# On-chip copies of keys by ScalarE and GpSimd in place of DMAs, later identities and a retuned order, in an attention and two-FFN kernel

## The chip, the cores and the metric

The kernel runs on one core of a Trainium2 chip. The metric is the device time of one execution in microseconds. Before the change the median of 3 runs is 525.11 us (524.25 to 525.11).

## The reference

Attention comes first: q, k and v are (2 batches, 8 heads, 768 positions, 64). Each query sees the keys of the last 128 positions, itself included, and the first 4 keys of its batch. Then two feed-forward blocks over the 1536 x 512 rows that result:

```python
scores = scale * q @ k.T; keep = is_sink | in_window
a = exp(scores - max); a = a / (sum(a) + 1e-9); x = a @ v      # heads side by side: 1536 x 512
h = x @ w_in                                                   # 512 -> 1024
solu = h * softmax(h)
ln = (solu - mean) / sqrt(var + 1e-6) * g_ln
x = ln @ w_out                                                 # 1024 -> 512
h = x @ w2_in                                                  # 512 -> 2048
r = relu(h); out = (r * r) @ w2_out                            # 2048 -> 512
```

Inputs and output are float32 arrays; the weights arrive as raw 64-bit words that the kernel converts on the chip.

## The kernel before, in words

**Precision.** A float32 operand is split into a high and a low float16 part, and a product is three matmuls (high by high, high by low, low by high). So every operand is prepared twice: ScalarE (ACT) or VectorE (DVE) writes the high part, TensorE (PE) subtracts it again with a scaled negative identity (`negq`, `neg1`, `negp`; lines L610, L476), and ACT or DVE writes what is left, the low part.

**Tiles.** There are 12 tiles of 128 queries, six to a batch, called t = 0 to 11. A tile's scores have up to 260 columns: its own 128 keys, 4 sink keys, and the 128 keys of the tile before. For each tile `prep_q` and `prep_k` turn q and k with transposes on PE (L592, L594) and build the tiles `qs` and `ks`, which hold high and low parts stacked over the two halves of the partitions. Tile 0 is built in halves by ACT from PSUM. For t = 1 and later the second halves are copies from partitions 64 to 127 into 0 to 63 or back: three DMAs of queries (L657, L659, L661; the third reads what the first writes), three of keys (L701, L703, L705), one 128 x 1024 DMA of the previous tile's keys (L714), and a small GpSimd (POOL) copy of the sink keys (L712). `prep_v` clips v and splits it (`vs`; L725 to L736). Then come the eight heads (scores L789, a custom DVE pass with the row's maximum L799, exponentials on ACT L804), the transposes of the probabilities, their split, the product with v (L866), and the division by the sums (`xs`, L886).

**First and second FFN.** `first(t)` (L957) multiplies the turned attention rows `xh`/`xl` by w_in, `norm(t)` forms solu and its moments (L1000 to L1020, with one power step on POOL, L1018, and the scaled result `so` by POOL, L1020), and `second(t)` (L1046) multiplies by w_out. Weights come in units: craw10 to craw13 for w_in, craw20 to craw23 for w_out, 1 MB each (L504, L506), which DVE converts in three passes of 128 x 1024 (L431, L433, L435); then ACT writes the high part and PE and ACT the low part (L475 to L478). The second FFN's units w3x follow the same way at about 255 us and later (low part by DVE, L466), in 16 steps of `h2` (L1080), `square` (L1093, `gh` L1097, `gl` L1100) and `o2` (L1117), each for four groups of columns. `gl` may go to DVE or POOL.

**Who sets the order.** The kernel's generators ask for an engine with an estimated time, and a list scheduler, `Order`, issues on the host the ask that can start earliest by these estimates; of asks that are ready by the time the engine is free the one with the lowest key goes first. The keys stand in the table at L32 to L50. All engines run their instructions in the order written, and SP issues nearly all DMAs, in order: an SP instruction that waits holds all DMAs behind it. The loads of tile 0's k and q have the fixed key -50; the load of gains is asked with key 0, a weight unit with its entry of `C_KEY`. The four scaled identities (L242) are made by POOL before everything that it is asked for later. `dg` (L563) are eight diagonal matrices on POOL that turn the gain into a matmul.

Of the kernel before, what the change touches and what calls it, by code (L numbers as in the profile page):

```python
# [17 lines left out]
ALU = mybir.AluOpType  # L18
# [13 lines left out]
PE_W = (17.45, 21.36, 14.67, 76.35, 72.53, 117.36, 72.01, 5.72)  # L32
PE_T = (-40.11, 93.82, 0.88, 1.8, -18.4)
LEAD = 41.26
C_KEY = (-13.78, -119.36, -163.11, -72.69, -17.51, -197.67, -111.51, 11.15)
W_AT = (-21.55, 118.65)
K_W = -173.85
K_HEAD = (6.34, 33.8, 152.98, 26.26)
K_TURN = (13.58, 52.57, -0.0)
K_PV = (32.41, -132.48)  # L40
K_PREPK = (-83.35, 152.22, -72.32)
K_PREPQ = (6.35, 247.73, 58.74)
K_PREPV = (38.93,)
K_LOAD = 119.08
K_FIRST = (-16.04, 28.03, 17.79)
K_NORM = 20.87
K_LNT = (-123.17, -36.52)
K_SECOND = (19.15, -1.15, -46.7)
A_0 = (-25.54, -32.74, -19.99, -9.44)
F_0 = (44.96, -4.33, -33.57, -14.12)  # L50
# [157 lines left out]
def attention_moe_moe2(ctx: ExitStack, tc: tile.TileContext, q, k, v, n_sink, window,  # L208
# [32 lines left out]
    for dst, by in ((negq, -1.0 / QSC), (idw, WSC), (neg1, -1.0), (negp, -1.0 / PSC)):  # L241
        nc.gpsimd.tensor_scalar(dst, ident, by, None, ALU.mult)  # L242
# [44 lines left out]
    with tc.manual_schedule():  # L287
# [182 lines left out]
        def low_w(l, x, h, by):  # L470

            for c in range(2):
                yield take("L")
                yield PE, 1.1
# [77 lines left out]
        def load_gsb():  # L552
# [7 lines left out]
            for i in range(CF):  # L560
                if PE_W[CM + i // 2] > 0:
                    yield POOL, 0.3
                    nc.gpsimd.tensor_scalar(dg[:, i], ident, gsw[:, i:i + 1], None, ALU.mult)  # L563
            post("dg")

# [40 lines left out]
        def low_part(t, kind, dst, tr, hi, by, scale=1.0):  # L606

            if less(t, kind):
                yield PE, 0.23
# [10 lines left out]
        HALVES = ((slice(0, 64), slice(64, 128), 0), (slice(64, 128), slice(0, 64), 1))  # L620

        def prep_q(t):
# [3 lines left out]
            for n, h0, h1 in parts(t):  # L626
# [5 lines left out]
                if t < NDIR:  # L632
                    yield ACT, 2 * act_us(512 * sh)
                    for r, o, a in HALVES:
                        nc.scalar.activation(qs[r, 0, a, ps_], tv[r], AF.Copy, scale=QSC)
                    yield PE, 0.3 * sh
# [19 lines left out]
            yield SP, 0.5  # L656
            nc.sync.dma_start(qs[0:64, :, 1], qs[64:128, :, 0])  # L657
            yield SP, 0.5, 2.0
            nc.sync.dma_start(qs[64:128, :, 1], qs[64:128, :, 0])  # L659
            yield SP, 0.5, 2.0  # L660
            nc.sync.dma_start(qs[64:128, :, 0], qs[0:64, :, 0])  # L661
            post(("q", t, 0))

        def prep_k(t):
# [8 lines left out]
            for n, h0, h1 in parts(t):  # L673
# [5 lines left out]
                if t < NDIR:  # L679
                    yield ACT, 2 * act_us(512 * sh)  # L680
                    for r, o, a in HALVES:
                        nc.scalar.activation((k0, k1)[a][r, ps_], tv[r], AF.Copy, scale=QSC)
                    yield PE, 0.3 * sh
# [10 lines left out]
            if t >= NDIR:  # L694
# [5 lines left out]
                yield SP, 0.5, 2.0  # L700
# [747 lines left out]
```

## Time and profile before

| what | value |
|---|---|
| median of 3 runs | 525.11 us |
| the profiled execution | 523.43 us, span 521.6 us |
| PE busy | 492.5 us, 94% of the span |
| DVE busy | 353.4 us, 68% |
| ACT busy | 297.8 us, 57% |
| POOL busy | 105.3 us, 20% |
| granted clock of PE | 0.996 of full speed on average |

The span is what the profiler saw of the core; 1.8 us of the execution lie outside it. Busy shares are averages over stages with different limits: in the first 80 us weights are converted while tiles 0 to 2 go through, in 80 to 260 us attention and the first FFN alternate on PE, around 260 to 280 us the kernel goes over to the second FFN, and from 280 us on there is the second FFN alone.

### The profile page before, as it was taken

The numbers are of one execution on the slowest core, as the hardware profiler recorded it, in microseconds if no ns is written. First come the engines' busy times: TensorE is split into PE (matmuls) and PEld (weight loads), VectorE is DVE, ScalarE is ACT, GpSimd is POOL, SyncE is SP. The second block draws the span as 40 slices with busy tenths as digits, with TensorE's granted clock in tenths as the row PEclk, the third lists the DMA queues.
The fourth block names the chain that finished last, engine by engine and source line by source line (L and its number), as shares of the span: only waits on it lengthen the run. The fifth ranks groups of instructions, "written<-read, shape, count | busy, mean of one in ns | idle before, by whom it ended". The sixth has DMA issues, their size and how long they took to land.

```text
span 521.6 us, 10644 instructions
## 1 busy us (share of the span) xinstructions
PE 492.5 (94%) x4022; PEld 317.1 (61%) x4022; DVE 353.4 (68%) x819; ACT 297.8 (57%) x658; POOL 105.3 (20%) x190
## 2 busy tenths in 40 slices
PE   4779989999999999999988999999999999999993
PEld 2345568878887888787764555555555555555551
DVE  3788958976776687689899898733475444763223
ACT  6768977777766776564534343567645655322221
POOL 3813753352604222122300000000000000110000
PEclk9999999999999999999999999999999999999998
DMA  6998794444353318003345444677889997000003
GB/s 177 303 268 246 151 233 91 95 92 92 78 113 84 85 42 271 1 18 109 119 147 177 162 165 165 234 268 280 321 313 333 372 330 243 0 2 1 1 0 128
DMA packets 91180, 82.31 MB, mean 158 GB/s; under 512 B 60656, under 2 KB 81264, under 8 KB 88944
## 3 DMA queue, kind: packets, MB, share of 16 engines
q1 hardware_dynamic: 90976, 81.55, 51.5%
q8 instruction: 33, 0.54, 0.5%
q14 instruction: 27, 0.22, 0.1%
q10 hardware_dynamic: 144, 0.00, 0.0%
HBM read 69.28 MB, written 3.15 MB: 139 GB/s over the span
## 4 chain that ended last, share of the span: by engine, by line
PE 80%; DMA 7%; DVE 5%; POOL 3%; ACT 2%; issue 1%; SPq 1%; POOLq 0%; DVEq 0%; ACTq 0%
PE ps L1080 24%; PE ps L1117 23%; PE ps L1046 10%; PE ps L957 10%; PE ps L594 6%; PE ps L789 3%; PE ps L866 3%; DMA craw<-in_moe_w_in_dram 2%; DMA craw<-in_moe_w_out_dram 2%; DMA vraw<-in_v_dram 1%; DVE cx L433 1%; DMA ks<-ks 1%; PE ps L592 1%; DMA qraw<-in_q_dram 1%; POOL vs L736 1%
## 5 line engine op out<-in xcount | busy, mean ns | idle before, releaser
L1093 DVE SCALAR_TENSOR_TENSOR gf<-ps,relu 128x384 f32<-128x384 f32 x64 | 35.5, 555 | 75.4 <-ACT relu L1090 70.8
L1090 ACT ACTIVATE relu<-ps 128x384 f32<-128x384 f32 x64 | 31.3, 489 | 92.4 <-PE ps L1080 92.4
L1080 PE MATMUL ps<-x2h,w34l 128*128 128x384 f16 x256 | 83.5, 326 | 0.0
L1080 PE MATMUL ps<-x2l,w34h 128*128 128x384 f16 x256 | 83.4, 326 | 0.0
L1080 PE MATMUL ps<-x2h,w34h 128*128 128x384 f16 x256 | 83.4, 326 | 0.0
L1080 PEld LDWEIGHTS <-w34h 128*128 128x128 f16 x512 | 49.7, 98 | 38.4
L1117 PE MATMUL ps<-w34h,gh 128*128 128x512 f16 x192 | 72.8, 379 | 0.0
L1117 PE MATMUL ps<-w34h,gl 128*128 128x512 f16 x192 | 72.8, 379 | 0.0
L1117 PE MATMUL ps<-w34l,gh 128*128 128x512 f16 x192 | 72.8, 379 | 0.0
L1046 PE MATMUL ps<-lnh,w2h 128*128 128x128 f16 x384 | 68.2, 219 | 1.3 <-DVE facb L1157 1.3
L1046 PE MATMUL ps<-lnl,w2h 128*128 128x128 f16 x384 | 68.1, 219 | 1.1 <-DVE lnl L616 1.1
L1046 PE MATMUL ps<-lnh,w2l 128*128 128x128 f16 x384 | 68.1, 219 | 0.0
L1046 PEld LDWEIGHTS <-w2h 128*128 128x128 f16 x768 | 61.3, 98 | 5.6 <-issue 1.7
L1117 PEld LDWEIGHTS <-gh 128*128 128x128 f16 x384 | 37.5, 98 | 38.6
L1100 POOL TENSOR_TENSOR gl<-gf,gh 128x384 f16<-128x384 f32 x10 | 9.6, 956 | 202.6 <-ACT gh L1097 202.6
L804 ACT ACTIVATE pp<-neg,bias_all 128x260 f32<-128x260 f32 (+1 forms) x96 | 46.9, 491 | 5.0 <-DVE bias_all L799 3.8
L1097 ACT CAST gh<-gf 128x384 f16<-128x384 f32 x64 | 32.5, 508 | 29.1 <-DVE gf L1093 29.1
L799 DVE CUSTOM_DVE_ANT_0 neg<-ps,m 128x260 f32<-128x260 f32 (+1 forms) x96 | 36.6, 397 | 14.5 <-PE ps L789 8.8
L1100 DVE TENSOR_TENSOR gl<-gf,gh 128x384 f16<-128x384 f32 x54 | 30.0, 556 | 19.6 <-ACT gh L1097 19.6
L1046 PEld LDWEIGHTS <-w2l 128*128 128x128 f16 x384 | 37.6, 98 | 1.2 <-issue 1.2
L789 PE MATMUL ps<-ks,qs 128*128 128x260 f16 (+1 forms) x192 | 35.5, 269 | 2.2 <-DVE bias_all L799 1.6
L957 PE MATMUL ps<-w1h,xh 128*128 128x512 f16 x96 | 36.4, 379 | 0.1
(230 smaller groups left out, 1020.7 us busy)
## 6 DMA issues: line engine op xcount, KB each, us to landing
craw<-in_moe_w_in_dram SPq DMA_DIRECT2D x16, 512.0 KB, 5.3
craw<-in_moe_w_out_dram SPq DMA_DIRECT2D x16, 512.0 KB, 4.7
qs<-qs SPq DMA_DIRECT2D x33, 128.0 KB, 3.4
craw<-in_moe_w_in_dram SPq DMA_DIRECT2D x4, 1024.0 KB
craw<-in_moe_w_out_dram SPq DMA_DIRECT2D x4, 1024.0 KB, 5.8
crawx<-in_q_dram SPq DMA_DIRECT2D x3, 1024.0 KB, 5.8
crawx<-in_k_dram SPq DMA_DIRECT2D x3, 1024.0 KB, 7.4
crawx<-in_v_dram SPq DMA_DIRECT2D x3, 1024.0 KB, 8.2
```

The costliest lines, as they stand in the source:

```text
L594: nc.tensor.transpose(out, src, ident)
L789: nc.tensor.matmul(o, QS[t][:, x, a, p, :], KS[t][:, a, p, 0:w], start=(x == 0), stop=(x == 1))
L799: nc.vector.tensor_tensor_reduce(neg[:, 0:w], o, m, scale=-0.125 / (QSC * QSC), scalar=3.0e38, op0=ALU.add, op1=ALU.min, accum_out=bias)
L804: nc.scalar.activation(pp[:, a, 0:w], neg[:, 0:w], AF.Exp, bias=bias, scale=-1.0, accum_out=SUMS[t][:, j:j + 1])
L957: nc.tensor.matmul(bank(B_H + hh), l[:, c, :], r[:, c, hh * 512:(hh + 1) * 512], start=(c == 0 and k == 0), stop=(c == CM - 1 and k == 2))
L1046: nc.tensor.matmul(o[:, ms], l[:, c, ms], ln[r][:, c % 4, :], start=(n == 0), stop=(n == 12 * CF - 1))
L1080: nc.tensor.matmul(o, l[:, c, :], r[gi][:, c, xs], start=(k == 0), stop=(k == 3 * CM - 1))
L1090: nc.scalar.activation(tt, o, AF.Relu, scale=G2SC / (X2SC * WSC) ** 2)
L1093: nc.vector.scalar_tensor_tensor(gf, o, 0.0, tt, ALU.max, ALU.mult, accum_out=gsum[:, n:n + 1])
L1097: nc.scalar.copy(gh, gf)
L1100: (nc.gpsimd if eng == POOL else nc.vector).tensor_tensor(gl, gf, gh, ALU.subtract)
L1117: nc.tensor.matmul(ps[:, ACC[m]], l[:, ms], r, start=(f == 0 and i == 0), stop=(f == CF2 - 1 and i == 2))
```

## The change

A new generator `move` copies within the chip. Its kind says what: 0 queries, 1 the tile's own keys, 2 the previous tile's keys. Below the threshold T_COPY[kind] for the tile number t it asks for ACT, DVE or POOL, whichever the scheduler can start first, else it issues a DMA as before. With the thresholds given, queries stay on DMA for all tiles, the own keys are copied by an engine for t = 1 alone (three copies of 64 x 512), and the previous tile's keys for all ten tiles that have one (128 x 1024). In the order that results the three copies of t = 1 stand on ACT and the ten of the previous keys on POOL. The identities are made by a step of their own behind POOL's index steps (`scaled`), and what reads them waits for it. The fixed key of tile 0's loads becomes K_LOAD0. The estimates for a DMA issue (0.5 to 0.65) and for `dg` (0.3 to 0.6) change, and so does every key in the table. All 64 `gl` stand on POOL in the new order (10 of 64 before, the others on DVE), and both steps of the low part of v on POOL for the two tiles that had it on DVE (L733).

```diff
-PE_W = (17.45, 21.36, 14.67, 76.35, 72.53, 117.36, 72.01, 5.72)
...
-C_KEY = (-13.78, -119.36, -163.11, -72.69, -17.51, -197.67, -111.51, 11.15)
...
+T_COPY = (-16.61, 1.23, 22.13)
+K_LOAD0 = -3.08
+PE_W = (59.84, 31.21, 13.49, 50.01, 33.64, 206.75, 96.92, 28.53)
...
+C_KEY = (-26.92, -150.49, -222.09, -92.67, 7.82, -175.79, -155.85, 9.24)
...
-    for dst, by in ((negq, -1.0 / QSC), (idw, WSC), (neg1, -1.0), (negp, -1.0 / PSC)):
-        nc.gpsimd.tensor_scalar(dst, ident, by, None, ALU.mult)
...
+        def scaled():
+            for dst, by in ((negq, -1.0 / QSC), (idw, WSC), (neg1, -1.0), (negp, -1.0 / PSC)):
+                yield POOL, 0.53
+                nc.gpsimd.tensor_scalar(dst, ident, by, None, ALU.mult)
+            post("scaled")
...
+        def move(t, kind, dst, src, n, last=True):
+
+            if t < T_COPY[kind]:
+                eng = yield (ACT, 0.2 + n * 0.00083), (DVL, 0.15 + n / 3840.0), (POOL, 0.2 + n * 0.001)
+                (nc.scalar.copy if eng == ACT else (nc.gpsimd if eng == POOL else nc.vector).tensor_copy)(dst, src)
+            else:
+                yield (SP, 0.65, 2.0) if last else (SP, 0.65)
+                nc.sync.dma_start(dst, src)
...
-                nc.sync.dma_start(k1[64:128], k0[64:128])
-                yield SP, 0.5
-                nc.sync.dma_start(k1[0:64], kl[64:128])
-                yield SP, 0.5, 2.0
-                nc.sync.dma_start(k0[64:128], kl[0:64])
+                yield from move(t, 1, k1[64:128], k0[64:128], 512)
+                yield from move(t, 1, k1[0:64], kl[64:128], 512, False)
+                yield from move(t, 1, k0[64:128], kl[0:64], 512)
...
-                yield SP, 0.75, 2.0
-                nc.sync.dma_start(ks[:, :, :, P + NSK:].rearrange("p a c n -> p (a c) n"), ks0[:, :, :, 0:P].rearrange("p a c n -> p (a c) n"))
+                yield from move(t, 2, ks[:, :, :, P + NSK:].rearrange("p a c n -> p (a c) n"), ks0[:, :, :, 0:P].rearrange("p a c n -> p (a c) n"), 1024)
...
+        start(-60.0, scaled())
...
-                    att(b + K_LOAD + n if t or nm == "v" else -50 + 3 * n + 4 * part[0], load(nm, src, t, *part))
+                    att(b + K_LOAD + n if t or nm == "v" else K_LOAD0 + 3 * n + 4 * part[0], load(nm, src, t, *part))
```

SP's first ten DMAs before; kraw0 and qraw0 are tile 0's keys and queries, in halves, par the window's size:

```order
L318 DMA kraw0_140<-in_k_dram 128x4x64
L323 DMA par_67<-in_window_dram 128x2
L318 DMA qraw0_141<-in_q_dram 128x4x64
L318 DMA kraw0_140<-in_k_dram 128x4x64
L318 DMA qraw0_141<-in_q_dram 128x4x64
L504 DMA craw10_157<-in_moe_w_in_dram 128x2048
L554 DMA gsb_93<-in_moe_g_ln_dram 128x8x1
L318 DMA kraw1_145<-in_k_dram 128x8x64
L318 DMA qraw1_146<-in_q_dram 128x8x64
L504 DMA craw11_217<-in_moe_w_in_dram 128x2048
```

The same ten places now:

```order
L323 DMA par_67<-in_window_dram 128x2
L505 DMA craw10_149<-in_moe_w_in_dram 128x2048
L318 DMA kraw0_136<-in_k_dram 128x4x64
L318 DMA qraw0_137<-in_q_dram 128x4x64
L555 DMA gsb_89<-in_moe_g_ln_dram 128x8x1
L318 DMA kraw0_136<-in_k_dram 128x4x64
L505 DMA craw11_167<-in_moe_w_in_dram 128x2048
L318 DMA qraw0_137<-in_q_dram 128x4x64
L318 DMA kraw1_141<-in_k_dram 128x8x64
L318 DMA qraw1_142<-in_q_dram 128x8x64
```

The first weight unit stands ahead of tile 0's keys, and the second one among tile 0's halves; in both the rows follow the program's start.

PE at the first heads of tile 1 before, with the semaphores that each row waits for; DMAHW names a DMA queue:

```order
L475 MATMUL ps_61<-cx12_334,idw_71 128x512 [waits Activation_49]
L476 LDWEIGHTS neg1_68
L476 MATMUL ps_61<-w1h_117,neg1_68 128x512
L592 MATMUL ps_61<-ident_62,kraw2_225 128x128 [waits DMAHW4_49]
L592 MATMUL ps_61<-ident_62,kraw2_225 128x128 x3
L789 LDWEIGHTS qs1_148 [waits DMAHW1_49,DMAHW7_49,DVE_49,DMAHW6_49]
L789 MATMUL ps_61<-ks1_147,qs1_148 128x260 [waits Pool_49]
L789 LDWEIGHTS qs1_148
L789 MATMUL ps_61<-ks1_147,qs1_148 128x260
```

The same place now:

```order
L801 LDWEIGHTS qs1_144 [waits DMAHW4_49]
L801 MATMUL ps_61<-ks1_143,qs1_144 128x260 [waits DVE_49]
L801 LDWEIGHTS qs1_144
L801 MATMUL ps_61<-ks1_143,qs1_144 128x260
L801 LDWEIGHTS qs1_144 [waits DMAHW1_49,DMAHW0_49]
L801 MATMUL ps_61<-ks1_143,qs1_144 128x260 [waits DVE_49]
L801 LDWEIGHTS qs1_144
L801 MATMUL ps_61<-ks1_143,qs1_144 128x260
L476 MATMUL ps_61<-cx12_352,idw_71 128x512 [waits DVE_49]
```

The heads stand ahead of the low part of unit craw12 (before: behind it and behind the transposes of kraw2, L592), and wait for fewer DMA queues: those of the queries alone.

POOL ahead of the power step of tile 0's norm (st0) before; vs4 is the split of tile 4's v, so0 the scaled result that PE turns next:

```order
L725 TENSOR_SCALAR vraw4_596<-vraw4_596 128x512
L810 COPY snk2_576<-pp2_2_751 128x4x4
L730 TENSOR_SCALAR vs4_784<-vraw4_596 128x512
L735 TENSOR_SCALAR vraw4_596<-vraw4_596 128x512
L736 TENSOR_TENSOR vs4_784<-vraw4_596,vs4_784 128x512
L1018 TENSOR_TENSOR st0_753<-st0_753,half_95 128x1
L810 COPY snk2_576<-pp2_2_751 128x4x4
L1020 TENSOR_SCALAR so0_808<-so0_808,st0_753 128x1024
```

The same place now, with the program's new line numbers (L1018 is L1030, L1020 is L1032):

```order
L737 TENSOR_SCALAR vraw4_580<-vraw4_580 128x512
L742 TENSOR_SCALAR vs4_755<-vraw4_580 128x512
L822 COPY snk2_591<-pp2_2_746 128x4x4
L747 TENSOR_SCALAR vraw4_580<-vraw4_580 128x512
L748 TENSOR_TENSOR vs4_755<-vraw4_580,vs4_755 128x512
L822 COPY snk2_591<-pp2_2_746 128x4x4
L822 COPY snk2_591<-pp2_3_805 128x4x4
L1030 TENSOR_TENSOR st0_707<-st0_707,half_91 128x1
L1032 TENSOR_SCALAR so0_815<-so0_815,st0_707 128x1024
```

The split of vs4 keeps its place ahead of the power step, and two copies of sink probabilities (snk2) came between them.

## Rows read from the trace of the kernel before

**Rows 1.** The page, busy time of each engine.

```profile
PE 492.5 (94%) x4022; PEld 317.1 (61%) x4022; DVE 353.4 (68%) x819; ACT 297.8 (57%) x658; POOL 105.3 (20%) x190
```

**Rows 2.** Busy time by stretch: start:end, length, engines, clock, DMA share, GB/s.

```profile
0.00:80.00 80.00, 63.17 (x440) 37.66 (x441) 59.82 (x146) 61.72 (x151) 40.99 (x75) 1.00 0.89 225
4.64:38.30 33.66, 23.89 (x118) 12.54 (x119) 25.19 (x65) 25.82 (x66) 13.88 (x19) 1.00 1.00 273
40.00:66.72 26.72, 25.58 (x181) 15.06 (x180) 24.74 (x51) 23.72 (x56) 12.78 (x17) 1.00 0.83 198
80.00:260.00 180.00, 179.36 (x2167) 145.46 (x2164) 138.87 (x360) 119.94 (x292) 55.64 (x108) 1.00 0.37 93
260.00:280.00 20.00, 16.13 (x159) 10.86 (x158) 19.79 (x30) 7.66 (x13) 2.20 (x2) 1.00 0.48 161
```

**Rows 3.** PE's waits in 0 to 80 us: total, times, longest.

```profile
PE ps L594 <- POOL so L1020: 1.7, 1, 1.7
```

**Rows 4.** Timeline of SP's queue, 0 to 63 us: start, length, DMA issued.

```profile
0.72 0.45 SPq L318 DMA_DIRECT2D kraw<-in_k_dram  x1
...
19.49 0.60 SPq L659 DMA_DIRECT2D qs<-qs  x1
...
20.77 0.70 SPq L504 DMA_DIRECT2D craw<-in_moe_w_in_dram  x1
25.91 0.60 SPq L661 DMA_DIRECT2D qs<-qs  x1
...
28.02 1.23 SPq L506 DMA_DIRECT2D craw<-in_moe_w_out_dram  x1
...
62.92 0.38 SPq L318 DMA_DIRECT2D vraw<-in_v_dram  x1
```

**Rows 5.** DMA issues of the whole run: times, size, median us to landing.

```profile
qs<-qs SPq DMA_DIRECT2D x33, 128.0 KB, 3.4
```

**Rows 6.** Timeline of PE: start, length, instruction, idle before and its releaser.

```profile
3.95 0.66 PE L592 MATMUL ps<-ident,kraw 128*128 128x128 f32 x2 [3.95 <-POOL mtmp L340]
...
31.56 0.39 PE L789 MATMUL ps<-ks,qs 128*128 128x260 f16 x2
...
39.72 0.38 PE L957 MATMUL ps<-w1h,xh 128*128 128x512 f16 x1
...
72.29 0.66 PE L594 MATMUL ps<-ident,so 128*128 128x128 f32 x4 [1.69 <-POOL so L1020]
```

**Rows 7.** Timeline of ACT.

```profile
8.46 0.82 ACT L646 COPY qs<-qs 64x256 f16<-64x256 f16 x2
...
38.30 0.58 ACT L935 CAST xh<-ps 128x512 f16<-128x512 f32 x1 [1.05 <-PE ps L592]
```

**Rows 8.** Timeline of DVE, 10 to 67 us.

```profile
10.92 0.69 DVE L431 TENSOR_SCALAR cx<-craw 128x1024 int32<-128x1024 int32 x1 [1.29 <-DMA craw<-in_moe_w_in_dram]
...
29.21 0.69 DVE L431 TENSOR_SCALAR cx<-craw 128x1024 int32<-128x1024 int32 x1 [0.89 <-DMA craw<-in_moe_w_in_dram]
...
31.20 1.23 DVE L435 SCALAR_TENSOR_TENSOR cx<-craw,cx 128x1024 int32<-128x1024 int32 x1
...
49.91 1.95 DVE L435 SCALAR_TENSOR_TENSOR cx<-craw,cx 128x1024 int32<-128x1024 int32 x1
...
66.72 0.15 DVE L1016 TENSOR_SCALAR st<-vart 128x1 f32<-128x1 f32 x1
```

**Rows 9.** Timeline of POOL, 48 to 72 us.

```profile
48.88 1.89 POOL L752 TENSOR_TENSOR svt<-svs,bd 128x512 f32<-128x512 f32 x1
...
66.87 0.61 POOL L725 TENSOR_SCALAR vraw<-vraw 128x512 f32<-128x512 f32 x1 [1.94 <-DMA vraw<-in_v_dram]
...
70.33 0.57 POOL L1018 TENSOR_TENSOR st<-st,half 128x1 f32<-128x1 f32 x1
...
71.04 1.20 POOL L1020 TENSOR_SCALAR so<-so,st 128x1024 f32<-128x1024 f32 x1
```

**Rows 10.** Timeline of DVE at the end of attention.

```profile
261.84 0.55 DVE L1100 TENSOR_TENSOR gl<-gf,gh 128x384 f16<-128x384 f32 x1
```

More of the change, by code (lines that the diff above doesn't have):

```diff
@@ L31 @@
 RAMP = 1
-PE_W = (17.45, 21.36, 14.67, 76.35, 72.53, 117.36, 72.01, 5.72)
-PE_T = (-40.11, 93.82, 0.88, 1.8, -18.4)
-LEAD = 41.26
-C_KEY = (-13.78, -119.36, -163.11, -72.69, -17.51, -197.67, -111.51, 11.15)
[L36 to L50, printed above, removed]
+T_COPY = (-16.61, 1.23, 22.13)
+K_LOAD0 = -3.08
+PE_W = (59.84, 31.21, 13.49, 50.01, 33.64, 206.75, 96.92, 28.53)
+PE_T = (-73.15, 112.32, 0.69, 1.96, -9.95)
+LEAD = 41.3
+C_KEY = (-26.92, -150.49, -222.09, -92.67, 7.82, -175.79, -155.85, 9.24)
+W_AT = (-88.34, 129.42)
+K_W = -129.94
+K_HEAD = (-17.11, 30.3, 105.37, -38.14)
+K_TURN = (14.13, 41.97, 30.04)
+K_PV = (32.72, -105.88)
+K_PREPK = (-105.13, 82.35, -39.58)
+K_PREPQ = (6.91, 238.1, 90.13)
+K_PREPV = (-4.93,)
+K_LOAD = 83.89
+K_FIRST = (-16.07, 27.92, 204.9)
+K_NORM = 46.99
+K_LNT = (-133.54, -19.26)
+K_SECOND = (18.84, -1.43, -46.23)
+A_0 = (-9.6, -55.61, -13.68, -3.07)
+F_0 = (26.35, -1.45, -50.35, -25.1)
 SLACK = 0.0
@@ L473, in low_w @@
                 yield take("L")
+                yield on("scaled")
                 yield PE, 1.1
@@ L561, in load_gsb @@
                 if PE_W[CM + i // 2] > 0:
-                    yield POOL, 0.3
+                    yield POOL, 0.6
                     nc.gpsimd.tensor_scalar(dg[:, i], ident, gsw[:, i:i + 1], None, ALU.mult)
             post("dg")
+        def scaled():
[3 more added lines that the diff above has]
+            post("scaled")
         QS, KS, VS, SV = {}, {}, {}, {}
@@ L608, in low_part @@
             if less(t, kind):
+                yield on("scaled")
                 yield PE, 0.23
@@ L635, in prep_q @@
                         nc.scalar.activation(qs[r, 0, a, ps_], tv[r], AF.Copy, scale=QSC)
+                    yield on("scaled")
                     yield PE, 0.3 * sh
@@ L655, in prep_q @@
             back(t, bk)
-            yield SP, 0.5
-            nc.sync.dma_start(qs[0:64, :, 1], qs[64:128, :, 0])
-            yield SP, 0.5, 2.0
-            nc.sync.dma_start(qs[64:128, :, 1], qs[64:128, :, 0])
-            yield SP, 0.5, 2.0
-            nc.sync.dma_start(qs[64:128, :, 0], qs[0:64, :, 0])
+            yield from move(t, 0, qs[0:64, :, 1], qs[64:128, :, 0], 1024, False)
+            yield from move(t, 0, qs[64:128, :, 1], qs[64:128, :, 0], 1024)
+            yield from move(t, 0, qs[64:128, :, 0], qs[0:64, :, 0], 1024)
             post(("q", t, 0))
@@ L682, in prep_k @@
                         nc.scalar.activation((k0, k1)[a][r, ps_], tv[r], AF.Copy, scale=QSC)
+                    yield on("scaled")
                     yield PE, 0.3 * sh
@@ L699, in prep_k @@
                 back(t, bk)
-                yield SP, 0.5, 2.0
-                nc.sync.dma_start(k1[64:128], k0[64:128])
-                yield SP, 0.5
-                nc.sync.dma_start(k1[0:64], kl[64:128])
-                yield SP, 0.5, 2.0
-                nc.sync.dma_start(k0[64:128], kl[0:64])
+                yield from move(t, 1, k1[64:128], k0[64:128], 512)
+                yield from move(t, 1, k1[0:64], kl[64:128], 512, False)
+                yield from move(t, 1, k0[64:128], kl[0:64], 512)
                 give("kl")
```

## The prediction, before the changed kernel was run

> **What bounds the kernel now.** I read the busy shares first: TensorE (PE) is busy for 492.5 us of a span of 521.6 [rows 1], so the most that a new order can give is what PE idles. The busy times by stretch say where that is [rows 2]. In 0 to 80 us PE is busy for 63.2 us and idle for 16.8. In 80 to 260 us it idles for 0.6 us in all: no DMA, no copy and no POOL step of that stretch is waited for, so whatever the change saves there is worth nothing. In 260 to 280 us it idles for 3.9 us while VectorE (DVE) is busy for 19.8 of 20: DVE is the limit there. The granted clock is 1.00 (2.4 GHz) in all five stretches, so a shift is a shift and not a change of speed. The reader should see that the change must pay before 80 us or not at all, apart from a little at 260.
>
> In the first 40 us the waits are many and small. DMA runs at a share of 0.89 over 80 us and at 1.00 from 4.64 to 38.30, at 273 GB/s [rows 2]: transfers wait for transfers there. craw13, the last w_in unit, is issued at 20.77 [rows 4] and DVE starts on it at 29.21, having waited for it last [rows 8]: 8.4 us for 1 MB. The third query copy of tile 1 is issued at 25.91, 6.4 us after the second one [rows 4], where the median landing of such a copy is 3.4 [rows 5]. After it come the first heads of tile 1 at 31.56, then the turned rows at 38.30 on ScalarE (ACT) [rows 7] and first(0) at 39.72 [rows 6]. The largest single wait with a name later on is 1.7 us for so0 [rows 3], at 72.29 [rows 6]: POOL began to split vraw4 at 66.87, waiting for its DMA, and came to the power step at 70.33 [rows 9], although DVE had delivered the operand at 66.72 [rows 8].
>
> **The change part by part**, against the profiled execution, 523.43 us: a span of 521.6 and 1.8 outside it. It lies 1.7 us below the median of the runs, so I take the sum as a difference and subtract it from 525.11.
>
> *Loads at the start (a cost).* craw10 now goes ahead of kraw0. Before, kraw0 is issued at 0.72 [rows 4] and PE turns it at 3.95 [rows 6]. Now it is third in the queue: about 1.1 us later from two more issues of some 0.5 each, and behind 1 MB, which at 273 GB/s [rows 2] takes 3.8 us of the DMA engines if nothing overlaps with its own latency. So the first transposes are 1.1 to 4.9 us late. I take 2.75, since part of the megabyte passes during kraw0's own 3.2 us of flight. In return DVE gets craw10 around 6 instead of 10.92 [rows 8].
>
> *The three key copies of tile 1 on ACT (a cost on ACT).* Two copies of 64x256 took 0.82 us, 0.41 each [rows 7]; 64x512 is at most twice that, so three cost 1.2 to 2.5 us. I take 1.5, as most of a short ACT instruction's time is not its elements. They replace DMAs that the heads waited for. But the queries stay on DMA, and the heads still wait for these; the key copies alone therefore bring nothing to the heads' start. What can is SP's order.
>
> *first(0) (the gain).* From 4.64 to 38.30 ACT is busy for 25.8 of 33.7 us [rows 2], idle for 7.8, of which the last 1.05 are for PE's transposes [rows 7] and stay. If the weights and copies come early enough to take the other 6.8 away, ACT reaches xh0 at 38.30 - 6.8 + 2.75 + 1.5 = 35.75, 2.5 us earlier. That they do I conclude from SP's order: craw13 now stands ahead of tile 1's query copies, so it can land at about 22 instead of 29, and with it the conversion and its low part leave the path; the third query copy stands behind craw20, and I reckon 28 to 29 for its landing and so for the heads. **I take -2.4 us at first(0)**, with bounds of +3.2 (the first rival) and -3.6 (the start costs only 1.1).
>
> *so0.* vraw4's DMA stands at row 40 of SP's order instead of 51, so the split of v is over before DVE reaches the norm, and the power step follows DVE's operand directly. 70.33 - 66.87 = 3.5 us of POOL's delay go; PE waited only 1.7 of it [rows 3]. **-1.7**, bounds 0 and -3.5. What is late next is DVE itself.
>
> *DVE in between (gives back).* From 40.00 to 66.72 DVE is busy for 24.74 of 26.72 us [rows 2]. A lead of 2.4 us at first(0) can't be carried through by an engine with 2.0 us of slack unless its own work moves up. Two low parts of v leave DVE (under 1.5 us) and the conversions begin earlier, which is why I give back only **+0.9**, bounds 0 and +3.0.
>
> *Copies of the previous keys and the splits on POOL.* Ten copies of 128x1024, by the nearest row at most 1.2 us each (so0's 128x1024 in float32 [rows 9]). POOL is busy for 41 of 80 us and 56 of 180 [rows 2], so the time itself is covered. It is the neighbourhood that costs: DVE's pass L435 takes 1.23 us alone [rows 8] and 1.95 at 49.91, started beside a POOL step that ran from 48.88 to 50.77 [rows 9]. Such two-input passes fill about 20 of the 56 us between 10.9 and 67 (16 passes of 1.23), a third; four new copies and two more splits there meet one about twice, at 0.7 each, half of it on the path. **+0.4 with what else meets**, bounds 0 and +1.6.
>
> The Trainium skill, "SBUF — State Buffer", section "Who interferes with whom", says that a DVE instruction with two SBUF inputs and a GpSimd instruction that reads SBUF exclude each other, and that the second waits for the whole of the first. The row agrees: 50.77 plus 1.23 is 52.0, and the pass ended at 51.86. By the rule a new copy could hold a DVE pass for all its 1.2 us, and the sum would have +1 to +2 here instead of +0.4; that speaks against putting copies on POOL, and is weighed in the second rival.
>
> *260 to 280.* One `gl` of 0.55 us [rows 10] leaves DVE where DVE is the limit: **-0.5**, bounds 0 and -0.55. The other 53 that move lie where PE is never short (in the last stage DVE's and POOL's work is well below PE's). *Identities:* POOL makes them a few steps later, still before PE's first low part, which has to wait for transposes and ACT: nothing, and if they came late, under 0.5 us of the start.
>
> **Sum:** -2.4 - 1.7 + 0.9 + 0.4 - 0.5 = -3.3 us, 521.8.
>
> **Rivals.** *Slower: tile 1's query copies hold PE.* In the new order the heads of tile 1 stand ahead of craw12's low part, so PE has nothing to do past them. If the copies are issued 1 us later than now for the late start, at 20.5, and the second again takes 6.4, the third is issued at 27 and queues behind craw20: 0.6 + 3.8 + 3.4 puts the heads at 34.8, 3.2 us later than 31.56. first(0) follows: +3.2 - 1.7 + 0.9 + 0.4 - 0.5 = +2.3, **527.4**. It decides once the heads start after about 32.5. For it: these copies are slow already [rows 4]; against it: three key DMAs are out of the queue, and craw13 has gone before. *No change: DVE eats the lead.* It keeps its 3.0 in the tight stretch and POOL's copies cost 1.6: -2.4 - 1.7 + 3.0 + 1.6 - 0.5 = 0, **525.1**. For it: 93% busy, and the lengthened passes. Against: DVE's idle time before 40 us (8.5 of 33.7) is there to be used by weights that come earlier. *More:* the start costs only 1.1, so0 comes the whole 3.5 earlier and DVE keeps up: -3.6 - 3.5 + 0.9 + 0.4 - 0.5 = -6.3, **518.8**.
>
> **How the numbers follow.** Forecast 0.50, with its own range of 519.8 to 523.8; more 0.15; no change 0.15; slower 0.20. A measurement tells about 0.2% (1.05 us) from no change. Faster takes the forecast, the larger gain and a little of the case of no change: 0.67; the same gets 0.12, slower 0.21. The range reaches from 518.0, just short of the large gain, to 526.8, which leaves out the worse half of the slower case.
>
> **What would show it.** Right: PE's first transposes at 6 to 7; craw13's first pass on DVE before 25; heads of tile 1 before 30.5; first(0) near 37.3; the power step of norm 0 within 0.5 us of DVE's operand, and the wait for so0 on PE gone; PE idle in 0 to 80 us at 13.5 to 14.5. Wrong: heads of tile 1 after 32.5 with a wait for a query DMA; or first(0) early but so0 not, with DVE back to back and passes of 1.9 us and more beside POOL's copies; or new PE waits in 80 to 260, for a POOL copy or split, where there is no slack.

## The result: slower by 6 us, and the profile after

The changed kernel takes 531.12 us (median of 4 runs, 529.73 to 531.92) against 525.11 (524.25 to 525.19): a ratio of 1.0109 with a 95% interval of 1.0082 to 1.0135, about 6 us slower. The forecast was 521.8, with a range up to 526.8. The profiled execution took 531.80 us, 8.4 more than that of before. The changed kernel's four runs had mean granted clocks of 0.984 to 0.996; what the clock has to do with the loss is weighed below.

The page's busy line, and the stretches that answer to [rows 1, 2] (columns as there):

```profile
PE 496.2 (94%) x4022; PEld 320.4 (60%) x4022; DVE 337.3 (64%) x763; ACT 299.9 (57%) x662; POOL 173.4 (33%) x257
```

```profile
0.00:80.00 80.00, 57.81 (x344) 33.15 (x345) 58.80 (x133) 57.47 (x140) 42.04 (x73) 0.94 0.80 207
80.00:260.00 180.00, 180.00 (x2191) 146.51 (x2190) 137.94 (x362) 122.93 (x300) 61.41 (x119) 1.00 0.31 80
260.00:280.00 20.00, 17.48 (x191) 14.08 (x189) 17.60 (x27) 8.13 (x13) 5.14 (x5) 0.91 0.40 132
```

PE's work is the same 4022 matmuls, but in the first 80 us it is busy for 57.8 us instead of 63.2, and at a clock of 0.94. From 80 to 260 us it has no idle time at all. Most of what is lost is lost before 80 us, where the forecast looked for the gain.

PE's longest waits in 0 to 80 us (total, times, longest), which answer to [rows 3]:

```profile
PE ps L599 <- DMA kraw<-in_k_dram: 10.4, 1, 10.4
PE ps L801 <- ACT ks L634: 2.9, 1, 2.9
```

The wait for so0 is gone from the list. In its place the first row is a wait of 10.4 us for tile 0's keys, at the very start. The second row names ACT's copies of keys, which the change put there. That name is a guess of the profile, and the rows below show that it is the wrong one: ACT's last copy ends at 24.24 us (22.98 plus 1.26), when PE has already gone on at 24.23.

The start of SP's queue, which answers to [rows 4] (start, length of the issue, DMA):

```profile
1.18 0.41 SPq L505 DMA_DIRECT2D craw<-in_moe_w_in_dram  x1
1.63 0.43 SPq L318 DMA_DIRECT2D kraw<-in_k_dram  x1
...
4.84 4.84 SPq L318 DMA_DIRECT2D kraw<-in_k_dram  x1
9.73 0.51 SPq L505 DMA_DIRECT2D craw<-in_moe_w_in_dram  x1
...
12.30 3.40 SPq L505 DMA_DIRECT2D craw<-in_moe_w_in_dram  x1
...
21.49 0.34 SPq L505 DMA_DIRECT2D craw<-in_moe_w_in_dram  x1
...
27.17 1.37 SPq L637 DMA_DIRECT2D qs<-qs  x2
```

The four units of w_in, craw10 to craw13, stand at 1.18, 9.73, 12.30 and 21.49; before, craw12 was issued here:

```profile
15.37 0.94 SPq L504 DMA_DIRECT2D craw<-in_moe_w_in_dram  x1
```

The next rows are from PE, and answer to [rows 6]:

```profile
10.36 0.66 PE L599 MATMUL ps<-ident,kraw 128*128 128x128 f32 x2 [10.36 <-DMA kraw<-in_k_dram]
...
24.23 0.48 PE L801 MATMUL ps<-ks,qs 128*128 128x128 f16 x4 [2.86 <-ACT ks L634]
...
36.34 0.61 PE L801 MATMUL ps<-ks,qs 128*128 128x260 f16 x4
...
49.03 0.38 PE L969 MATMUL ps<-w1h,xh 128*128 128x512 f16 x1
...
79.16 0.60 PE L601 MATMUL ps<-ident,so 128*128 128x128 f32 x4
...
254.94 0.33 PE L1092 MATMUL ps<-x2h,w34h 128*128 128x384 f16 x1
```

The last of these places, the second FFN's first matmul, in the kernel before:

```profile
248.11 0.33 PE L1080 MATMUL ps<-x2h,w34h 128*128 128x384 f16 x1
```

kraw0, third in the queue at 1.63, is turned at 10.36, 6.4 us later than before; the second half of it is held on SP for 4.8 us until 9.68, and with it craw11 behind it. The lag at later places is 4.8 us at tile 1's heads (36.34), 6.6 at the turned rows xs0, 9.3 at first(0) (49.03), 6.9 at so0 (79.16) and 6.8 at the second FFN's first matmul (254.94). So it shrinks and grows again on the way, and ends near the size that it had at the first transposes. The other 1.6 of the 8.4 us between the two profiled executions are lost behind 254.94.

DVE, which answers to [rows 8] (L811 is the heads' pass, L664 the writing of query parts, L1028 the norm's last step):

```profile
9.82 0.69 DVE L431 TENSOR_SCALAR cx<-craw 128x1024 int32<-128x1024 int32 x1 [0.57 <-DMA craw<-in_moe_w_in_dram]
...
16.54 0.29 DVE L811 CUSTOM_DVE_ANT_0 neg<-ps,m 128x128 f32<-128x128 f32 x1 [4.76 <-PE ps L801]
...
22.62 1.22 DVE L664 COPY qs<-qs 64x256 f16<-64x256 f16 x2
...
24.10 0.08 DVE L811 DVE_READ_ACCUMULATOR2_ANT bias_all<- 128x1 f32 x1
...
32.91 0.69 DVE L431 TENSOR_SCALAR cx<-craw 128x1024 int32<-128x1024 int32 x1
...
36.03 0.68 DVE L431 TENSOR_SCALAR cx<-craw 128x1024 int32<-128x1024 int32 x1
...
76.38 0.14 DVE L1028 TENSOR_SCALAR st<-vart 128x1 f32<-128x1 f32 x1
```

The first head and the start on craw12 in the kernel before:

```profile
9.34 0.29 DVE L799 CUSTOM_DVE_ANT_0 neg<-ps,m 128x128 f32<-128x128 f32 x1 [0.53 <-PE ps L789]
...
24.09 0.69 DVE L431 TENSOR_SCALAR cx<-craw 128x1024 int32<-128x1024 int32 x1 [0.28 <-DMA craw<-in_moe_w_in_dram]
```

craw10 is there at 9.82, only 1.1 us earlier than before although it was issued 2.2 us earlier, ahead of everything but the broadcast. Its passes stand ahead of the first head, which comes at 16.54 (9.34 before). The conversion of craw12 starts at 32.91, behind heads 4 to 7, and was at 24.09 before; that of craw13 starts at 36.03, 6.8 us later than in [rows 8].

These rows also show what PE waits for at 24.23. DVE's pass over the scores of the head before is read out from 24.10 to 24.18, and PE goes on 0.05 us later. In the runs below the same matmul follows DVE's read-out by 0.05 to 0.06 us too (19.43 and 19.49 with craw10 third, 19.08 and 19.13 with all halves first), and there the profile names DVE for it. So the wait is for DVE, which had passes on craw10 and craw11 and two copies of query parts ahead of that head.

ACT's copies and POOL's power step (this answers to [rows 7, 9]):

```profile
22.34 0.61 ACT L634 COPY ks<-ks 64x512 f16<-64x512 f16 x1
22.98 1.26 ACT L634 COPY ks<-kl 64x512 f16<-64x512 f16 x2
```

```profile
18.09 1.04 POOL L634 COPY ks<-ks 128x1024 f16<-128x1024 f16 x1
...
70.92 0.61 POOL L737 TENSOR_SCALAR vraw<-vraw 128x512 f32<-128x512 f32 x1 [2.05 <-DMA vraw<-in_v_dram]
...
76.60 0.57 POOL L1030 TENSOR_TENSOR st<-st,half 128x1 f32<-128x1 f32 x1 [0.91 <-DVE st L1028]
```

A copy of 64x512 took 0.61 to 0.63 us on ACT: the three make 1.9, above the 1.5 that were taken and within the bounds. One of 128x1024 took 1.04 on POOL here, but another, at 67.09, took 1.50, above the bound of 1.2. The power step now waits for DVE (0.9 us idle), not the other way round.

### The profile page after: what moved, and what is told of

Same layout as the page of the kernel before. It is cut to its first block, busy times and chain, and to the rows that moved or that the text cites. A ratio compares the mean times of both kernels' runs of the same rounds, so it can differ in the third digit from the quotient of the medians.

```text
span 530.0 us, 10682 instructions
## 1 busy us (share of the span) xinstructions
PE 496.2 (94%) x4022; PEld 320.4 (60%) x4022; DVE 337.3 (64%) x763; ACT 299.9 (57%) x662; POOL 173.4 (33%) x257
## 4 chain that ended last, share of the span: by engine, by line
PE 88%; DVE 4%; ACT 3%; DMA 2%; issue 1%; SPq 0%; DVEq 0%; ACTq 0%
PE ps L1092 24%; PE ps L1129 23%; PE ps L1058 12%; PE ps L969 12%; PE ps L601 7%; PE ps L801 3%; PE ps L878 3%; PE ps L476 2%; DMA kraw<-in_k_dram 2%; PE ps L599 1%; PE ps L618 1%; DMA out_dram<-ob 0%; PE ps L477 0%; DVE cx L433 0%; PE ps L888 0%
## 5 line engine op out<-in xcount | busy, mean ns | idle before, releaser
L1112 POOL TENSOR_TENSOR gl<-gf,gh 128x384 f16<-128x384 f32 x64 | 67.5, 1056 | 192.4 <-ACT gh L1109 186.9
L1058 PE MATMUL ps<-lnh,w2h 128*128 128x128 f16 x384 | 69.5, 222 | 1.3 <-ACT lnh L947 1.3
L1058 PE MATMUL ps<-lnl,w2h 128*128 128x128 f16 x384 | 69.4, 222 | 1.2 <-DVE lnl L624 1.2
L1058 PE MATMUL ps<-lnh,w2l 128*128 128x128 f16 x384 | 69.4, 222 | 0.0
L811 DVE CUSTOM_DVE_ANT_0 neg<-ps,m 128x260 f32<-128x260 f32 (+1 forms) x96 | 37.0, 400 | 22.4 <-PE ps L801 15.8
L969 PE MATMUL ps<-w1l,xh 128*128 128x512 f16 x96 | 36.4, 379 | 0.0
```

Source lines behind the costliest of these rows:

```text
L811: nc.vector.tensor_tensor_reduce(neg[:, 0:w], o, m, scale=-0.125 / (QSC * QSC), scalar=3.0e38, op0=ALU.add, op1=ALU.min, accum_out=bias)
L969: nc.tensor.matmul(bank(B_H + hh), l[:, c, :], r[:, c, hh * 512:(hh + 1) * 512], start=(c == 0 and k == 0), stop=(c == CM - 1 and k == 2))
L1058: nc.tensor.matmul(o[:, ms], l[:, c, ms], ln[r][:, c % 4, :], start=(n == 0), stop=(n == 12 * CF - 1))
L1112: (nc.gpsimd if eng == POOL else nc.vector).tensor_tensor(gl, gf, gh, ALU.subtract)
```

## The experiments

Times are medians. Two theories were set against each other first. S: a megabyte ahead of tile 0's keys holds the start, and that is the loss. C: the on-chip copies and the order around them are the loss.

**SP's order alone, in the changed kernel.** craw10's DMA is held back until qraw0's first half is issued; every other engine's order stays.

```diff
+            if (nm, t, n) == ("q", 0, 0):
+                nc.sync.dma_start(held[0], wi1[0:P, :])
...
-            r = words(units[n])
+            if n == 0:
+                r = cp.tile([P, 2048], I32, tag="craw", name="craw10", bufs=3)
+                held.append(r)
+            else:
+                r = words(units[n])
```

> The changed kernel with one thing moved: the DMA of craw10 is issued behind tile 0's first halves of k and q instead of ahead of them; every other engine's order stays. Theory S (the megabyte ahead of tile 0's keys holds the first transposes, 10.4 us instead of 3.95, and the 6.4 us are never regained): first transposes at 4 to 5 us, and the time falls by 4 to 6 us, to 525 to 527. Rival C (the copies on ACT and POOL, 2.9 us of PE waiting for ACT's copies alone, with the order around them, make the loss; the late start is absorbed by later waits): first transposes early too, but the time stays at 529 to 531.

525.62 us against 524.81 for the kernel before (ratio 1.0018, 0.9989 to 1.0048): of the 6 us about 5 come back. The first transposes are at 5.67, the second FFN begins at 249.45.

```profile
5.67 0.66 PE L606 MATMUL ps<-ident,kraw 128*128 128x128 f32 x2 [5.67 <-DMA kraw<-in_k_dram]
```

**SP's order alone, in the kernel before.** craw10's DMA is issued first of all.

```diff
+            if (nm, t, n) == ("k", 0, 0):
+                held.append(words(units[0]))
...
-            r = words(units[n])
+            r = words(units[n]) if n else held[0]
```

> The kernel before with craw10's DMA issued first of all, nothing else changed. Theory S: first transposes at about 10 us and the time up by 4 to 6.5 us, to 529 to 531.5. Rival C: the later waits absorb it, 525 to 527.

529.22 against 524.81 (1.0095, 1.0063 to 1.0128): 4.4 us from one DMA moved. The first transposes are at 7.73, 3.8 late and not the 6 that were expected, and the second FFN is 3.4 late.

```profile
7.73 0.66 PE L595 MATMUL ps<-ident,kraw 128*128 128x128 f32 x2 [7.73 <-DMA kraw<-in_k_dram]
```

S stands so far: the start's lag is carried through nearly one to one. The megabyte by itself costs the first transposes 3.8 us; in the changed kernel they are 6.4 late, with par's broadcast ahead of the megabyte as well.

**All on-chip copies as DMAs**, in the changed kernel.

```diff
-                (nc.scalar.copy if eng == ACT else ...)(dst, src)
+                nc.sync.dma_start(dst, src)
```

> The changed kernel with all thirteen on-chip copies of keys (three on ACT, ten on POOL) issued as DMAs at the same places of the program; the order of everything else stays. Theory S: the first transposes stay at 10.4, the time stays within 1.5 us of the changed kernel, 529.5 to 532. Rival C: 2 to 4 us faster, 527 to 529, as the wait of 2.9 us on ACT's copies goes.

532.56 against 524.81 (1.0161, 1.0129 to 1.0193): not faster, if anything slower than the changed kernel. PE's second wait stays, at the same instruction, though ACT has no copies of keys any more; the profile now gives it another name:

```profile
PE ps L801 <- ACT w1h L460: 2.0, 1, 2.0
```

Here too PE goes on 0.05 us behind DVE's read-out (23.22 and 23.27). Tile 1's heads come at 40.2 instead of 36.3, as the DMAs are late in their turn. So DMAs in the copies' places are no better, and the wait that C was built on is not that of the copies. What else the copies may cost this run can't say.

**The key -50 restored**, so that the scheduler plans anew.

```diff
-K_LOAD0 = -3.08
+K_LOAD0 = -50.0
```

> The changed kernel with the key of tile 0's loads back at -50, so that the scheduler itself puts all halves of k and q ahead of craw10; the other engines' order follows anew. Theory S: 523 to 527. Rival C: 528 to 531, since the copies and the rest of the table stay.

535.48 (1.0213, 1.0183 to 1.0243). Both expectations are missed: the transposes are at 4.34, but with one key changed the scheduler writes another order for every engine. The second FFN's first matmul comes at 252.91, 4.8 us late, and more is lost behind it. A key of such a table can't be tested by changing it alone; the other runs hold the order fixed.

**kraw0 ahead of par, and all halves first**, in the changed kernel. Par is a broadcast of 128 x 2 words. The first run sends kraw0, par, qraw0, craw10; the second one kraw0, par, qraw0, both second halves, craw10, as before.

```diff
+            if n:
+                for x in (("k", 0),):
+                    send(*x)
             eng.dma_start(par[:, 2 * n:2 * n + 2], src.bitcast(I32).partition_broadcast(P))
+            if n:
+                for x in (("q", 0),):   # second run: (("q", 0), ("k", 4), ("q", 4))
+                    send(*x)
```

> The changed kernel with SP's start in the order kraw0, par, qraw0, craw10: against the run with craw10 third, only the first half of kraw0 now stands ahead of par, the broadcast of the window's size; all other engines keep the changed order. Theory P (the small broadcast at the head of the queue itself costs the next load 1.7 us: before, with kraw0 first, data move from 2.0 us on, with par first from 3.2): first transposes at about 4 us, the time 1 to 2 us below the run with craw10 third. Rival (the transposes at 5.7 came late because craw10 shares the DMA engines with kraw0): still 5 to 6 us, and the same time.

> The changed kernel with SP's first seven DMAs in the order of the kernel before: kraw0, par, qraw0, both second halves, craw10, gsb; the rest of the changed order on all engines stays. Theory S (all loss is at the start): first transposes at 4 us and a time of 523 to 525.5, level with the kernel before or below it. If the rest of the changed order loses by itself (DVE's heads 4 to 7 ahead of craw12's conversion), 526 to 528.

PE in the first of them:

```profile
3.95 0.66 PE L614 MATMUL ps<-ident,kraw 128*128 128x128 f32 x2 [3.95 <-DMA kraw<-in_k_dram]
...
10.42 0.66 PE L614 MATMUL ps<-ident,kraw 128*128 128x128 f32 x2 [2.52 <-DMA kraw<-in_k_dram]
```

The transposes come at 3.95 instead of 5.67, so kraw0's place behind the small broadcast had cost 1.7 us; but the time is 529.95 (1.0104, 1.0071 to 1.0138), 1.2 below the changed kernel's and 4.3 above that with craw10 third. The expectation has the transposes right and the time wrong. The second half, now behind craw10, is turned at 10.42 after a wait of 2.5. With all halves first the time is 525.27 (1.0011, 0.9987 to 1.0036). So the first transposes' time is not the whole measure, as S had it. What the first of these runs loses against the one with craw10 third, whose second half is turned at 9.91, stays open.

**DVE's order at the start.** In the changed order craw10's first two passes stand ahead of heads 0 and 1. One run does that alone in the kernel before, another undoes it in the run with all halves first.

```diff
+            if (t, j) == (0, 0):     # kernel before: both passes ahead of head 0
+                two()
...
+            if (t, j) == (0, 1):     # changed order: both passes behind head 1
+                kept.pop()()
```

> The kernel before with one thing changed, on DVE alone: the first two conversion passes of craw10 stand ahead of tile 0's first head, as they do in the changed order; SP's order stays. Theory D (the changed order ties tile 0's first head to craw10's landing, so that restoring SP's order alone gives back only part): the first head on DVE goes from 9.3 to about 13 us and the time up by 1 to 3.5 us, 526 to 528.5. Rival (the first heads have slack; only the transposes' start counts): within 0.7 us of the kernel before.

> The changed kernel with SP's first seven DMAs as before (the run with all halves first) and DVE's first two passes on craw10 behind heads 0 and 1 of tile 0. Theory D: the first head at 9 to 10.5 us instead of 12.5, the time 1 to 3 us below the run with all halves first, 522.5 to 524.5, which would beat the kernel before. Rival (the middle of the order loses: craw12's conversion behind heads 4 to 7): the head comes earlier and the time stays at 525 to 526.

DVE in the run with all halves first, where the tie is still there:

```profile
10.59 0.69 DVE L446 TENSOR_SCALAR cx<-craw 128x1024 int32<-128x1024 int32 x1 [3.76 <-DMA craw<-in_moe_w_in_dram]
...
12.46 0.28 DVE L826 CUSTOM_DVE_ANT_0 neg<-ps,m 128x128 f32<-128x128 f32 x1
```

The keys are there at 3.95 and the head is at 12.46. In the kernel before the tie costs 1.3 us (525.94 against 524.65; 1.0024, 1.0002 to 1.0046), which lies between the two expectations. Undone in the changed order it brings the head to 10.93 and the time to 526.78 (1.0040, 1.0020 to 1.0060): no gain. There theory D falls. The time lies 1.5 us above that of all halves first, and above the rival's range too; why is not shown.

**The copies in the kernel before**: both kinds, POOL's alone, ACT's alone.

```diff
-                nc.sync.dma_start(k1[64:128], k0[64:128])        # and the other two of t = 1
+                (nc.scalar.copy if t == 1 else nc.sync.dma_start)(k1[64:128], k0[64:128])
-                nc.sync.dma_start(ks[:, :, :, P + NSK:]..., ks0...)
+                nc.gpsimd.tensor_copy(ks[:, :, :, P + NSK:]..., ks0...)
```

> The kernel before with its copies made on chip at the same places of the program: tile 1's three own-key copies by ACT, all ten previous-key copies by POOL; nothing else changed. As predicted, tile 1's heads still wait for the query copies: they start within 1 us of 31.56, and the time stays within 1 us of the kernel before (524 to 526). Rival: fewer DMAs let the query copies and weights land 2 us earlier, 522 to 523.5.

> The kernel before with the ten copies of previous keys by POOL at the same places; tile 1's own keys stay on DMA. If POOL's copies are what cost in the run with both kinds of copies (526.9 against 524.9), 526 to 527.5; if ACT's three copies are, 524.5 to 525.5.

> The kernel before with tile 1's three own-key copies on ACT at the same places, the previous keys on DMA as before. POOL's copies alone cost nothing (524.8 against 524.7), both together 2 us; so 526 to 527.5. If the two only cost together, 524.5 to 525.5.

Both: 526.90 (1.0045, 1.0022 to 1.0068). POOL's alone: 524.76 (1.0002, 0.9978 to 1.0025). ACT's alone: 524.33 (1.0006, 0.9983 to 1.0029). Each kind by itself is worth nothing measurable. Both together cost about 2 us, more than either expectation had, and tile 1's heads come at 33.1. The two kinds were not taken out together in the changed order with the start restored, so part of C stands untested there.

**ACT's copies undone in the changed order** (halves first, own keys by DMA), and **craw12's passes ahead of heads 4 to 7**:

```diff
-                (nc.scalar.copy if eng == ACT else ...)(dst, src)
+                (nc.sync.dma_start if kind == 1 else nc.gpsimd.tensor_copy)(dst, src)
...
+            if (t, j) == (0, 4):     # craw12's three passes, in a free buffer
+                three()
```

> The changed kernel with SP's first seven DMAs as before (the run with all halves first, 525.3), and tile 1's three own-key copies as DMAs at the same places instead of on ACT; POOL's copies stay. If ACT's copies are what keeps the changed order from its gain, 1.5 to 2.5 us faster, 523 to 524; if the DMAs are late in their turn (as in the run with all copies by DMA), 525.5 to 527.

> The run with all halves first, and craw12's three passes on DVE ahead of heads 4 to 7 of tile 0 instead of behind them, in a buffer of their own. If the late conversion of craw12 (27.1 us instead of 24.1) is what holds first(0), the passes come at 21 to 23 us, xh0 2 us or more earlier, and the time falls to 522.5 to 524; if it isn't, 525 to 526.5.

525.68 (1.0012, 0.9988 to 1.0035) and 524.64 (0.9990, 0.9965 to 1.0015), where the run with all halves first had 525.27. ACT's copies by themselves are not it. With the conversion at 22.7 instead of 27.1 ACT comes to xh0 2.2 us earlier (40.10 against 42.34), but the time falls by 0.6 only, less than the runs can tell.

**gl on DVE again**, in the run with craw10 third.

```diff
-            (nc.gpsimd if eng == POOL else nc.vector).tensor_tensor(gl, gf, gh, ALU.subtract)
+            nc.vector.tensor_tensor(gl, gf, gh, ALU.subtract)
```

> The run with craw10 third, and all 64 low parts gl made by DVE instead of POOL, at the same places. If POOL's slower gl (1.06 us instead of 0.56) costs at the transition or in the tail, 0.5 to 1 us faster than the run with craw10 third; if it is hidden, within 0.5 us; if it had helped DVE at the transition as predicted, 0.5 us slower.

526.66, a ratio to the kernel before of 1.0018 (0.9995 to 1.0041). It is 1.0 us above the run with craw10 third: between hidden and a gain of POOL's, and too close to say.

**The power step.** In the kernel before, POOL's split of tile 4's v is written behind tile 0's power step and scaling.

```diff
+            do = later.append if t == 4 else (lambda f: f())   # prep_v(4): kept
...
+            if t == 0:                                         # norm(0): issued behind so0
+                for f in later:
+                    f()
```

> The kernel before with one thing changed, on POOL alone: the split of tile 4's v stands behind the power step and the scaling of tile 0's norm instead of ahead of them. As predicted for this term: the wait of 1.7 us of PE for so0 goes, and the time falls by 1.0 to 1.7 us, to 523.2 to 524. Rival (DVE is late right behind it, or the wait moves to tile 4's v): the wait goes and the time stays within 0.5 us.

522.69 against 524.65 (0.9974, 0.9950 to 0.9998): 2.0 us faster by the medians and 0.1 to 2.6 by the interval, and the only version whose interval lies below the kernel before. POOL and PE in it (L1021 is the power step):

```profile
66.02 0.57 POOL L1021 TENSOR_TENSOR st<-st,half 128x1 f32<-128x1 f32 x1 [1.62 <-DVE st L1019]
...
66.98 1.19 POOL L1023 TENSOR_SCALAR so<-so,st 128x1024 f32<-128x1024 f32 x1
68.25 0.61 POOL L727 TENSOR_SCALAR vraw<-vraw 128x512 f32<-128x512 f32 x1
```

```profile
69.51 0.60 PE L595 MATMUL ps<-ident,so 128*128 128x128 f32 x4
```

The power step starts 0.1 us after DVE's operand (65.79; in this execution 0.9 earlier than before), PE turns so0 at 69.51 without waiting, and tile 4's split starts at 68.25 and is not missed.

**The norm's last step earlier**, in the changed order, where DVE reaches it at 71.9 us (66.7 before) with heads, low parts and craw23's passes inside the norm. Here it stands four DVE steps earlier; the second run has craw12's passes early as well.

```diff
             nc.scalar.activation(e, so, AF.Square, ..., accum_out=vart[:, t:t + 1])
+            if t == 0:     # last DVE step, power step and scaling, issued here
+                rest()
```

> The run with all halves first (525.3) with one step moved: the last DVE step of tile 0's norm stands four DVE steps earlier (ahead of two heads, craw23's last pass and a low part), and the power step and scaling on POOL directly behind it in time. Theory N (in the changed order DVE reaches that step at 71.9 us instead of 66.7, and this takes the place of POOL's delay that the change removed): so0 comes 2 to 2.5 us earlier and the time falls by 1 to 2.5 us, to 523 to 524.3. Rival (DVE as a whole is the limit there, and what is moved behind is waited for instead): the step comes earlier and the time stays within 0.7 us of 525.3.

> The same move in the run with craw12's passes ahead of heads 4 to 7 (524.6). Theory N: 522.5 to 523.7, below the kernel before. Rival: 524 to 525.3.

DVE and POOL in the first of them:

```profile
69.69 0.15 DVE L1044 TENSOR_SCALAR st<-vart 128x1 f32<-128x1 f32 x1 [0.77 <-ACT e L1040]
```

```profile
69.92 0.57 POOL L1045 TENSOR_TENSOR st<-st,half 128x1 f32<-128x1 f32 x1
70.61 2.13 POOL L1046 TENSOR_SCALAR so<-so,st 128x1024 f32<-128x1024 f32 x1
```

The step does come 2.2 us earlier, but the times are 527.31 (1.0043, 1.0019 to 1.0066) and 525.58 (1.0019, 1.0001 to 1.0037): theory N falls. In the changed order PE does not wait for so0, so nothing can be had there. The first run is even 2.0 us above that of all halves first, more than the rival allowed; the scaling of so0 takes 2.13 us in it, and what the rest is stays open.

## Why the prediction was wrong

*Loads at the start.* This step failed by its size. Taken at +2.75, with +4.9 as the worse bound, the first transposes came +6.4 late. The sum had a megabyte at the rate of a running queue, 3.8 us, and for par's broadcast nothing but the slot of its issue. The runs part the two. The megabyte alone costs 3.8 us in the old order, just the sum's figure (7.73 against 3.95). The broadcast ahead of kraw0 costs 1.7 more (5.67 against 3.95). Together that is 5.5 of the 6.4. The trace after shows the DMA engines idle for four us and slow in the next, with the broadcast and craw10 issued at 0.72 and 1.18:

```profile
0.00:4.00 4.00, 0.00 (x0) 0.00 (x0) 0.67 (x3) 1.28 (x1) 3.43 (x19) 1.00 0.01 0
4.00:5.00 1.00, 0.00 (x0) 0.00 (x0) 0.00 (x0) 0.00 (x0) 0.10 (x1) 1.00 0.22 66
5.00:6.00 1.00, 0.00 (x0) 0.00 (x0) 0.00 (x0) 0.00 (x0) 0.00 (x0) 1.00 0.61 238
```

In the kernel before with craw10 first, ahead of the broadcast, data move from 1.6 us on:

```profile
1.60:2.00 0.40, 0.00 (x0) 0.00 (x0) 0.23 (x1) 0.40 (x1) 0.40 (x2) 1.00 1.71 266
```

The step was also priced for kraw0 alone: SP's next issue waits 4.8 us, and the second halves come late too. The first head is 7.2 us late, the last head of tile 0 4.7 (32.69 against 28.03), so only a part of the lag is made good. The two runs that move this DMA alone give its price, 4.4 us in the old order and about 5 in the new.

*first(0), -2.4.* Wrong, and this is where the sign was lost. It expected 6.8 us of ACT's idle time ahead of xh0 to go. ACT reaches xh0 at 44.90, where the sum had 35.75, and from its first step at 11.05 it is still idle for 7.3 us, where it had been idle for 7.8:

```profile
11.05:44.90 33.85, 23.80 (x113) 12.60 (x112) 23.48 (x50) 26.51 (x67) 19.17 (x27) 0.90 0.94 267
```

The step rested on craw13 landing at 22 because its row in SP's order stands ahead of the query copies. Its row moved up, but its issue did not (21.49 against 20.77 [rows 4]): SP waits 3.7 us for DVE's pass L435 to free a buffer. The query copies behind it are issued at 27.17 only, after a wait of 5.3 us for DVE's query parts. The issue of craw12 began 3.1 us earlier than before (12.30 against 15.37; it took 3.4 us, so it ended 0.6 earlier), and craw12 was converted 8.8 us later, since DVE's order has heads 4 to 7 ahead of it now, which the prediction didn't look at. It read times from the rows of an order.

The heads of tile 1 came at 36.34, at the late place that the first rival named, but PE had no wait for a query copy there: it came late itself. With the old start restored they come at 33.4, later than 31.56, and there the rival's wait does show, with 2.7 us. So the rival had the direction, and its wait only behind the main price. (The bound of -3.6 does not follow from the step's own terms: a start of 1.1 gives 34.10 for xh0, so -4.2. That changes a gain that did not come.)

*so0, -1.7.* PE no longer waits for so0, as forecast, but by luck. vraw4's DMA is issued at 66.14, not earlier than before (62.92), and POOL still waits for it, 2.05 us, until 70.92. What changed is that DVE comes to the norm's last step only at 76.38, 9.7 us later than before, when the split is long over. With all halves first it is the same: POOL begins the split at 66.44 after a wait of 1.99, before 66.87, and DVE comes at 71.90. That the delay on POOL has a price the run with the power step first shows, with about 2 us in the old order; here PE and DVE were late by 6.9 us, and there was no wait left to remove. *DVE in between, +0.9:* too small; the norm's last step is 9.7 us later than before, 5.2 with the start restored.

*Copies on POOL, +0.4.* Alone, in the old order, they cost nothing measurable. A DVE pass of two inputs does lengthen beside one: L433 takes 2.08 us from 18.12 on, beside POOL's copy of 18.09 to 19.13, against 1.23 alone. The Trainium skill, "SBUF — State Buffer", section "Who interferes with whom", says that a DVE instruction with two SBUF inputs contends with a GpSimd instruction that reads SBUF. The row agrees: 19.13 plus 1.23 is 20.36, and the pass ended at 20.20. In the changed order this pass stands on the chain of DVE that PE waits for at 24.23; what it cost there was not measured. *The three copies on ACT:* 1.9 us instead of 1.5. *260 to 280, -0.5:* not seen; PE is busy there for 17.5 of 20 us instead of 16.1, but partly at half the clock. With craw10 third and with all halves first, at a clock of 1.00 there, it is busy for 16.0 us. *Identities:* nothing, as forecast.

*The clock.* The forecast took 1.00 for granted. Behind PE's wait of 2.9 us [the second row of the waits above] the granted clock stood at 0.50 (1.2 GHz) for a while:

```profile
25.60:31.00 5.40, 4.73 (x11) 2.00 (x10) 2.14 (x8) 3.86 (x12) 3.17 (x5) 0.50 0.41 91
```

The kernel before shows no such stretch until its tail; the changed one has two more, from 45.34 and from 270.62, of 3.4 us each. (A column of 1.00 is not the whole truth either: near the start of the kernel before a matmul of 128x512 takes 0.63 us at 14.34, as the one at 29.22 in the stretch of 0.50 above, and 0.38 at 16.31.) Over the 272 runs on record, each against the mean of its own kernel, a run whose mean clock is 0.01 lower is about 1.7 us longer (an estimate from their times and clocks, 1.2 to 2.2 at 95%). The changed kernel's runs have a mean clock of 0.988 and the kernel before 0.993, so about 0.9 of the 6 us go with the clock. Whether the clock or the waits ahead of it make them, these runs can't part.

*Still open:* why the rest of the changed order, with the start restored, is level with the kernel before and not below it. From 40 to 90 us PE is then busy for 47.9 us against 47.2 before, so it is not there; in the first 40 us it is busy for 23.9, partly at half the clock, against 26.0. ACT's copies, craw12's conversion, DVE's tie at the start and the norm's last step were each undone alone, and none gives it back. One thing that the traces show and no run undid alone: ACT's order puts the three key copies and a weight's high part ahead of tile 1's query high part, which comes at 21.22 instead of 16.25 with all halves first, and DVE waits 1.7 us for it before the query copies can be issued (22.55 against 18.84).

## What to carry to other kernels

In this kernel the small loads that PE needs first had to go ahead of every large one: a broadcast and a megabyte ahead of them cost 6.4 us at the first transposes, and most of that was carried to the end. A DMA that moved up in the issue order gained nothing where its buffer or the engine that uses it came no earlier: follow these, not the row. The engine that a wait's row names is a guess: compare the end of its instruction with the end of the wait before a theory is built on it, as that of ACT's copies was here. Before a whole table is changed, try the one wait that the trace names and move the one step that causes it; here that gave about 2 us where the table cost 6.

## What the hardware showed that was not expected

A broadcast of 128 x 2 words at the head of the queue costs the load behind it 1.7 us (first transposes at 5.67 with it ahead of kraw0, 3.95 with it behind), of which only 0.46 is the later issue (1.18 against 0.72). A load of 1 MB issued behind that broadcast took 8.6 us from issue to first use (1.18 to 9.82); issued ahead of it, at 0.72, its data moved from 1.6 us on.
